# One planner task for both products' chunks of an out tile while attention runs, and two pacing constants of weight narrowing lowered

## The chip, the cores and the metric

The kernel runs on one core of one Trainium2 chip, with float32 inputs and outputs. The metric is the device time of one execution in microseconds; the median of three runs of the kernel before is 704.17 us (703.85 to 704.71).

## What is computed

Three parts follow one another, the output of each being the input of the next. Cut to what matters:

```python
scores = where(causal, -1e9, scale * q @ k.T + minimum(bias, 0))    # 2 x 8 heads, 576 tokens, 64 wide
attn = softmax(scores) @ v                                          # -> x, 1152 tokens x 512
for e in range(4):                                                  # first layer
    h = maximum(x @ w1[e], 0)                                       # 512 -> 1024
    y += p[:, e:e+1] * (h @ w2[e])                                  # 1024 -> 512
g = y @ w_gate                                                      # second layer, 512 -> 1536
out = (g * sigmoid(g) * (y @ w_val)) @ w_out
```

## The kernel before, in words

Large products run on TensorE in a reduced float32 format. To keep float32's precision, each operand is split into a high part and a low part, and a product is three matmuls: high by high, high by low, low by high. `xh` and `xl` are the parts of attention's output, `wah` and `wal` those of an inward weight, `woh` and `wol` of an outward weight, `hh` and `hl` of hidden values. A split is a cast to the high part (lines 326 and 330) and a subtraction for the low part (line 339).

The layers are cut into stages. A stage is one unit of 256 hidden columns for a range of tokens: first the inward products, whose results become hidden values, then `outof` (lines 1170 to 1211), which makes an out tile for every 128 tokens. An out tile sums two chunks of 128 hidden columns (NF = 2), three matmuls each (lines 1184 to 1186), and is then added to `acc_a` or `acc_b` (line 1282 on VectorE, line 1278 on ScalarE for the first).

Inward products have two forms. While attention runs, stages are direct (`into`, lines 1022 to 1024): 256 tokens (EARLY) until the first part of attention is there, 512 (HALF) later. A direct stage of 512 tokens has 24 matmuls of 512 columns. Afterwards a stage is a scheme of seven half-size products (lines 1123 to 1125; the sums of the parts on VectorE are lines 1142 and 1163); for 512 tokens that is 42 matmuls of 256 columns. It needs sums of token halves of x (line 1062, tiles `te` and `tt`), which are formed during and right after attention.

Attention, a pair of heads at a time: scores (lines 534 to 549, of which 546 and 549 use 64 rows of the array), bias and row extremes on VectorE (line 568), exponentials on ScalarE (line 577), reciprocals (line 584), normalization on ScalarE (line 334) or GpSimd (line 336) into `ns`, transposes on TensorE (line 628), and the products with the values (line 687).

Second-layer weights are narrowed to a form that is cheap to split: 36 halves, each loaded (line 776), passed through two operations on ScalarE (lines 784, 791) and three on VectorE (lines 788, 794, 797), and stored to memory (line 801).

The order of all of it is set when the program is built. Every piece of work is a task with a cost, its needs and a rank (`Plan.step`), and the planner always takes the task that can start first, then the one of lower rank; the order in which it takes tasks is each engine's instruction order. Work for the planner comes from `jobs` and `stages` (lines 1438 to 1513). `feed` asks for the next stage while fewer than six tasks of TensorE's dense work are open, so the size of a task says how much work is open. `jobs` yields direct stages as long as attention isn't done ("h" not in `late`) and records them in `part`; then it sets the pace of narrowing, and `stages` takes halves by it:

```python
late["pace"] = 2 * n1 - len(part) + sum(t1 < HALF for t1 in part) - CALM - REST
...
if "h" in late:
    passed += 1
    while late["made_n"] * late["pace"] < (passed - CALM) * 36:
        ...
        x[0].make(x[1])
        late["made_n"] += 1
```

Here n1 is 16, the number of first-layer units, and `passed` counts stages after attention. In the kernel before, `part` has five stages (three of 256 tokens, two of 512), so the pace is 32 - 5 + 3 - 5 - 5 = 20.

Of the kernel before, what the change touches and what calls it, by code (L numbers as in the profile page):

```python
# [18 lines left out]
P = 128  # L19
# [4 lines left out]
PIECES = 2  # L24
# [27 lines left out]
TADD = "vp"  # L52
THIGH = "av"
TLOW = "vp"
REST = 5
CALM = 5
LEAD = 6.0
ISSUE = 0.45
DMA_KB = 0.0033
# [53 lines left out]
def pe(c):  # L113
    return max(c / 2400 + 0.015, 0.109)
# [49 lines left out]
class Plan:  # L164
# [8 lines left out]
    def add(self, eng, cost, run=None, deps=(), take=(), give=(), rank=0.0, port="p", mode="r"):  # L173
        t = Task(eng, cost, run, [d for d in deps if d is not None], take, give, rank, port, mode)
        if not t.missing:
            self.ready.append(t)
        return t
# [102 lines left out]
def attention_moe_swiglu(ctx, tc, q_early, q_late, k, v, s, dp, w1, w2, wg, wv, wo, out):  # L280
# [4 lines left out]
    NT, _, DM = out.shape  # L285
# [6 lines left out]
    NF = FU // P  # L292
# [20 lines left out]
    late = {}  # L313
# [4 lines left out]
    def ring(name, n=2):  # L318
        return rings.setdefault(name, Ring(n))
# [606 lines left out]
    def bank(tag):  # L926

        have = [(psw, {"h": 2, "o": 1}[tag])]
        if "ps" in late:
            have.append((late["ps"], {"h": 3, "o": 2}[tag]))  # L930
        order = [p for i in range(4) for p, n in have if i < n]
        p = order[turns[tag] % len(order)]
        turns[tag] += 1
        return p.tile([P, BANK], F32, name=tag, tag=tag, bufs=dict((id(a), n) for a, n in have)[id(p)])
# [55 lines left out]
    def dense_pe(cost, run, deps, **kw):  # L990
        count["rank"] += 1
        t = add("pe", cost, run, list(deps) + [last_pe["t"]], rank=count["rank"], **kw)
        last_pe["t"] = t
        t.dense = True
        open_pe.append(t)
        return t
# [173 lines left out]
    def order(st):  # L1170

        return [t for t in ORDER if st.t0 <= t * P < st.t1]
# [3 lines left out]
    def outof(w, st, t, evac, split=False):  # L1176
        box = {}
        ts = slice(t * P - st.t0, t * P - st.t0 + P)

        def three(f, y, check=False):  # L1180
            op = box["p"][:, y]
            wh, wl = w.ops
            hh, hl = st.hid
            nc.tensor.matmul(op, hh[:, f, ts], wh[:, f, y], start=f == 0, stop=False, skip_group_check=check)  # L1184
            nc.tensor.matmul(op, hh[:, f, ts], wl[:, f, y], start=False, stop=False, skip_group_check=check)  # L1185
            nc.tensor.matmul(op, hl[:, f, ts], wh[:, f, y], start=False, stop=f == NF - 1, skip_group_check=check)  # L1186

        def item(f):
            def run():
                if f == 0:  # L1190
                    box["p"] = bank("o")
                three(f, slice(0, DM), split)

            def make(last):
                deps = w.done[:-(-(f + 1) * PIECES // NF)] + [x for (ff, c0, n), x in st.lows.items() if ff <= f and c0 < (t + 1) * P and c0 + n > t * P]
                give = []
                if f == NF - 1 and t == order(st)[-1]:
                    give = [(st.first, st.ring)] + ([(w.first, w.parts_ring)] if last else [])
                if f == NF - 1 and split:
                    for y in sides:  # L1200
                        evac(dense_pe(3 * pe(DM // 2), lambda y=y: three(f, y, True), deps), box["t"], lambda: box["p"], y)
                    return
                x = dense_pe(3 * pe(DM), run, deps, take=[] if f else [ring("o")], give=give)
                if f == 0:
                    box["t"] = x
                    x.note = lambda: setattr(plan, "filler", None)
                if f == NF - 1:
                    evac(x, box["t"], lambda: box["p"])
                return x
            return make  # L1210
        return [item(f) for f in range(NF)]

    left = {t: n1 for t in range(NT)}
    fresh = set(range(NT))
# [52 lines left out]
    def moe1_out(w, st, e):  # L1267
        items = []

        for t in order(st):  # L1270
            def evac(x, taker, bank_, t=t):
                new = t in fresh
                fresh.discard(t)

                def run(on="v"):
                    sc = pr[:, t, e:e + 1]
                    if on == "a":
                        nc.scalar.mul(acc(t), bank_(), sc)
                    elif new:
                        nc.vector.tensor_scalar(acc(t), bank_(), sc, None, op0=ALU.mult)  # L1280
                    else:
                        nc.vector.scalar_tensor_tensor(acc(t), bank_(), sc, acc(t), op0=ALU.mult, op1=ALU.add)  # L1282

                a = add(choices("av", "bank", DM) if new else "dve", None if new else 0.74, run,
                        [x, last_acc.get(t), late["gates"]], give=[(taker, ring("o"))], rank=prompt())
                last_acc[t] = a
                left[t] -= 1
                if left[t] == 0:
                    turn_x(t, a)
            items += outof(w, st, t, evac)  # L1290
        return items
# [129 lines left out]
    def moe2_out(w, st, first, last):  # L1421
        items = []
        for t in order(st):
            split = last and st.t0 > 0 and t == order(st)[-1]

            def evac(x, taker, bank_, y=slice(0, DM), t=t, split=split):
                def run(on="v"):
                    if first:
                        move(on, acc(t), bank_())
                    else:  # L1430
                        nc.vector.tensor_tensor(acc(t)[:, y], bank_()[:, y], acc(t)[:, y], op=ALU.add)
                deps = [x, last_acc.get(t)] + (turning[st.t0]["turned"] if first else [])
                c = y.stop - y.start
                a = add(choices("av", "bank", c) if first else "dve", None if first else dve(c), run, deps,
                        give=[] if split else [(taker, ring("o"))], rank=prompt())
                last_acc[t] = a
                if last:
                    add("dma", (0.48, 0.00143 * c), lambda: nc.sync.dma_start(out[t, :, y], acc(t)[:, y]), [a], rank=0)
            items += outof(w, st, t, evac, split)
        return items  # L1440

    def jobs():
# [15 lines left out]
        late["last"] = w_in[-1]  # L1458
        late["pace"] = 2 * n1 - len(part) + sum(t1 < HALF for t1 in part) - CALM - REST
        for i in range(i, n1):  # L1460
# [10 lines left out]
    def stages():  # L1471
# [3 lines left out]
        for i, t0, t1, lastone in jobs():  # L1475
# [12 lines left out]
# [3 lines that stand above are left out]
                    x = next(halves_n, None)  # L1491
# [145 lines left out]
```

## Time and profile before

| what | us |
|---|---|
| median of three runs | 704.17 |
| profiled execution | 702.54 |
| span of that execution | 700.7 |
| TensorE (PE) busy | 690.0 |
| weight loads of TensorE (PEld) busy | 600.8 |
| VectorE (DVE) busy | 539.8 |
| GpSimd (POOL) busy | 463.4 |
| ScalarE (ACT) busy | 356.2 |

The span runs from the first to the last instruction of the profiled execution; 1.84 us of its time lie around it. TensorE's matmuls are pipelined and their ends are modelled, so its busy time is an upper estimate, and the distances between starts tell more. The DMA engines moved 78.45 MB and were busy for between none and eight tenths of a slice. Attention lasts to about 124 us, the first layer to about 495 us, and the second layer takes the rest.

### The profile page before, as it was taken

To read this page: it belongs to the slowest core of one execution; us is meant where nothing else is said; L and a number is where in the kernel's file an instruction comes from. 1 tells how busy PE (TensorE), PEld (TensorE's weight loads), DVE (VectorE), ACT (ScalarE), POOL (GpSimd) and SP (SyncE) were. 2 spreads that over 40 slices of the span, in tenths; PEclk is the share of its full clock that TensorE was granted. 3 is DMA by queue.
4 is the path that set the end of the run, shared out by engine and by line. 5 is a ranking of instruction groups with operands and counts; after the bars stand their busy time and mean duration, and the time that the engine had idled before them with its cause. 6 is when DMAs were issued, how large, how long until landed. Compare 5 with 4: busy or idle time off the path is not lost.

```text
span 700.7 us, 11844 instructions
## 1 busy us (share of the span) xinstructions
PE 690.0 (98%) x4240; PEld 600.8 (86%) x4240; DVE 539.8 (77%) x1080; ACT 356.2 (51%) x751; POOL 463.4 (66%) x456
## 2 busy tenths in 40 slices
PE   8999999999999999999999999999999999999997
PEld 6766667788898989898989889988989999999996
DVE  7876756761678898999899998786876777787665
ACT  7888766233454555555646655455555333323110
POOL 3888726673465867577658677699998848484211
PEclk9999999999999999999999999999999999999999
DMA  6785541211144336534545465312022111000003
GB/s 201 256 286 207 156 150 34 64 62 68 47 150 151 123 119 196 174 112 162 185 132 173 177 195 166 102 38 88 1 75 77 61 31 61 32 31 1 1 1 135
DMA packets 30187, 78.45 MB, mean 112 GB/s; under 512 B 3488, under 2 KB 8096, under 8 KB 30128
## 3 DMA queue, kind: packets, MB, share of 16 engines
q1 hardware_dynamic: 29984, 77.56, 33.8%
q8 instruction: 33, 0.54, 0.3%
q14 instruction: 26, 0.21, 0.1%
q10 hardware_dynamic: 144, 0.13, 0.1%
HBM read 65.85 MB, written 11.83 MB: 111 GB/s over the span
## 4 chain that ended last, share of the span: by engine, by line
PE 89%; ACT 4%; DVE 4%; DMA 2%; issue 1%; SPq 0%; DVEq 0%; ACTq 0%
PE o L1184 13%; PE o L1185 12%; PE o L1186 12%; PE h L1123 12%; PE h L1124 12%; PE h L1125 12%; PE po L687 3%; PE tp L628 2%; PE h L1022 2%; PE h L1024 2%; PE h L1023 2%; ACT ns L577 2%; PE sp L546 2%; DVE tt L1062 1%; PE sp L534 1%; DMA d<-rows 1%
## 5 line engine op out<-in xcount | busy, mean ns | idle before, releaser
L1142 DVE TENSOR_TENSOR cc<-cc,h 128x320 f32<-128x320 f32 (+1 forms) x282 | 126.4, 454 | 51.5 <-PE h L1125 43.4
L1184 PE MATMUL o<-woh,hh 128*128 128x512 f32 x397 | 157.4, 396 | 0.4 <-DVE acc_a L1282 0.3
L1186 PE MATMUL o<-woh,hl 128*128 128x512 f32 x397 | 155.0, 390 | 1.1 <-DVE hl L339 1.1
L1185 PE MATMUL o<-wol,hh 128*128 128x512 f32 x397 | 155.8, 392 | 0.0
L339 POOL TENSOR_TENSOR wal<-raw,wah 128x512 fp32r<-128x512 f32 (+1 forms) x58 | 72.7, 1263 | 34.4 <-ACT wah L326 33.0
L1123 PE MATMUL h<-xh,wsh 128*128 128x320 f32 (+1 forms) x312 | 92.8, 297 | 0.1
L1125 PE MATMUL h<-xh,wsl 128*128 128x320 f32 (+1 forms) x312 | 92.4, 296 | 0.0
L1124 PE MATMUL h<-xl,wsh 128*128 128x320 f32 (+1 forms) x312 | 92.4, 296 | 0.0
L1186 PEld LDWEIGHTS o<-woh,hl 128*128 128x128 f32 x397 | 74.6, 188 | 17.9 <-DVE hl L339 1.5
L339 POOL TENSOR_TENSOR hl<-cc,hh 128x512 fp32r<-128x512 f32 (+1 forms) x29 | 43.5, 1499 | 70.2 <-ACT hh L1254 70.1
L1184 PEld LDWEIGHTS o<-woh,hh 128*128 128x128 f32 x397 | 74.6, 188 | 13.2 <-DVE acc_b L1282 0.8
L339 POOL TENSOR_TENSOR wol<-raw,woh 128x512 fp32r<-128x512 f32 x54 | 77.0, 1441 | 11.8 <-ACT woh L326 10.9
L1185 PEld LDWEIGHTS o<-wol,hh 128*128 128x128 f32 x397 | 74.6, 188 | 10.6
L1251 ACT ACTIVATE cc<-cc 128x640 f32<-128x640 f32 (+1 forms) x46 | 32.2, 699 | 87.9 <-DVE cc L1142 87.9
L1123 PE MATMUL h<-xh,wah 128*128 128x320 f32 (+1 forms) x234 | 69.5, 297 | 0.9 <-DVE cc L1142 0.9
L1124 PE MATMUL h<-xl,wah 128*128 128x320 f32 (+1 forms) x234 | 69.2, 296 | 0.0
L1125 PE MATMUL h<-xh,wal 128*128 128x320 f32 (+1 forms) x234 | 69.2, 296 | 0.0
L339 POOL TENSOR_TENSOR wsl<-sf,wsh 128x512 fp32r<-128x512 f32 x44 | 64.2, 1478 | 2.2 <-ACT wsh L326 2.2
L1282 DVE SCALAR_TENSOR_TENSOR acc_b<-o,pr,acc_b 128x512 f32<-128x512 f32 x75 | 55.5, 744 | 7.0 <-PE o L1186 7.0
L1123 PEld LDWEIGHTS h<-xh,wsh 128*128 128x128 f32 x312 | 58.8, 188 | 1.9 <-ACT cc L326 0.3
L1124 PEld LDWEIGHTS h<-xl,wsh 128*128 128x128 f32 x312 | 58.6, 188 | 1.4
L1125 PEld LDWEIGHTS h<-xh,wsl 128*128 128x128 f32 x312 | 58.6, 188 | 0.0
(156 smaller groups left out, 1631.9 us busy)
## 6 DMA issues: line engine op xcount, KB each, us to landing
raw<-in_w SPq DMA_DIRECT2D x42, 512.0 KB, 5.0
n<-hl SPq DMA_DIRECT2D x36, 256.0 KB, 2.3
raw<-n SPq DMA_DIRECT2D x18, 512.0 KB, 3.3
hh<-in_wg SPq DMA_DIRECT2D x12, 512.0 KB, 4.2
hh<-in_wv SPq DMA_DIRECT2D x12, 512.0 KB, 3.9
hh<-in_wo SPq DMA_DIRECT2D x12, 512.0 KB, 3.8
dql<-rows SPq DMA_DIRECT2D x8, 512.0 KB, 4.0
vr<-in_v SPq DMA_DIRECT2D x4, 640.0 KB, 4.5
```

The costliest lines, as they stand in the source:

```text
L339: {"v": nc.vector, "p": nc.gpsimd}[e].tensor_tensor(to, x, f32(y), op=ALU.subtract)
L546: nc.tensor.matmul(sp[j][:, at:at + w], Q[half[j], x], K[half[j], :w], start=True, stop=False)
L687: nc.tensor.matmul(po[half[j], lo - a:e - a], raw[self.pi // 2]["v"][:kn, c, two + j * D:two + j * D + D], self.spot(self.p[j], c, lo, e, ...
L1123: nc.tensor.matmul(hp, wh, h, start=c == 0, stop=False)
L1124: nc.tensor.matmul(hp, wh, l, start=False, stop=False)
L1125: nc.tensor.matmul(hp, wl, h, start=False, stop=c == 1)
L1142: nc.vector.tensor_tensor(part(k), part(x), banks[i], op=ALU.add)
L1184: nc.tensor.matmul(op, hh[:, f, ts], wh[:, f, y], start=f == 0, stop=False, skip_group_check=check)
L1185: nc.tensor.matmul(op, hh[:, f, ts], wl[:, f, y], start=False, stop=False, skip_group_check=check)
L1186: nc.tensor.matmul(op, hl[:, f, ts], wh[:, f, y], start=False, stop=f == NF - 1, skip_group_check=check)
L1251: nc.scalar.activation(src()[:, o], src()[:, o], AF.Relu)
L1282: nc.vector.scalar_tensor_tensor(acc(t), bank_(), sc, acc(t), op0=ALU.mult, op1=ALU.add)
```

## The change

Two constants are lowered, and `outof` puts both chunks of an out tile, six matmuls, into one task of the planner while attention runs; after attention there is a task for each chunk as before.

```diff
--- before.py
+++ after.py
@@ -52,8 +52,8 @@
 TADD = "vp"
 THIGH = "av"
 TLOW = "vp"
-REST = 5
-CALM = 5
+REST = 4
+CALM = 3
 LEAD = 6.0
 ISSUE = 0.45
 DMA_KB = 0.0033
@@ -1185,30 +1185,32 @@
             nc.tensor.matmul(op, hh[:, f, ts], wl[:, f, y], start=False, stop=False, skip_group_check=check)
             nc.tensor.matmul(op, hl[:, f, ts], wh[:, f, y], start=False, stop=f == NF - 1, skip_group_check=check)
 
-        def item(f):
+        def item(f, e):
             def run():
                 if f == 0:
                     box["p"] = bank("o")
-                three(f, slice(0, DM), split)
+                for x in range(f, e):
+                    three(x, slice(0, DM), split)
 
             def make(last):
-                deps = w.done[:-(-(f + 1) * PIECES // NF)] + [x for (ff, c0, n), x in st.lows.items() if ff <= f and c0 < (t + 1) * P and c0 + n > t * P]
+                deps = w.done[:-(-e * PIECES // NF)] + [x for (ff, c0, n), x in st.lows.items() if ff < e and c0 < (t + 1) * P and c0 + n > t * P]
                 give = []
-                if f == NF - 1 and t == order(st)[-1]:
+                if e == NF and t == order(st)[-1]:
                     give = [(st.first, st.ring)] + ([(w.first, w.parts_ring)] if last else [])
-                if f == NF - 1 and split:
+                if e == NF and split:
                     for y in sides:
                         evac(dense_pe(3 * pe(DM // 2), lambda y=y: three(f, y, True), deps), box["t"], lambda: box["p"], y)
                     return
-                x = dense_pe(3 * pe(DM), run, deps, take=[] if f else [ring("o")], give=give)
+                x = dense_pe(3 * (e - f) * pe(DM), run, deps, take=[] if f else [ring("o")], give=give)
                 if f == 0:
                     box["t"] = x
                     x.note = lambda: setattr(plan, "filler", None)
-                if f == NF - 1:
+                if e == NF:
                     evac(x, box["t"], lambda: box["p"])
                 return x
             return make
-        return [item(f) for f in range(NF)]
+        step = 1 if "h" in late else NF
+        return [item(f, f + step) for f in range(0, NF, step)]
 
     left = {t: n1 for t in range(NT)}
     fresh = set(range(NT))
```

With the order that results, `part` has six stages (three of 256 tokens, three of 512), and the pace is 32 - 6 + 3 - 3 - 4 = 22. From line 1213 on, line numbers are higher by two (1282 is 1284, 1235 is 1237, 1278 is 1280).

The first place is TensorE's, in attention between two groups of scores; `sp` are scores, `po` the products with the values, `tp` transposes, `o` an out tile. The piece is of the difference between the two orders:

```order
 L1185 MATMUL o<-wol,hh 128x512
 L1186 MATMUL o<-woh,hl 128x512
+L1184 MATMUL o<-woh,hh 128x512
+L1185 MATMUL o<-wol,hh 128x512
+L1186 MATMUL o<-woh,hl 128x512
+L687 MATMUL po<-p,vr 64x320 x6
+L687 MATMUL po<-p,vr 64x192 x2
+L687 MATMUL po<-p,vr 64x64 x2
 L546 MATMUL sp<-k_108,ql 128x512 x2
 L549 MATMUL sp<-tri,idr 128x128 x2
 L549 MATMUL sp<-tri,idr 128x64 x2
```

The second chunk of the tile follows the first at once, and the products with the values, which came after the next scores, come ahead of them.

The second place is ScalarE's, at the cast of a sum of token parts (`xh` from `te`) in attention; `st` with a number is a head pair's row statistics. Before:

```order
L334 ACTIVATE ns<-ns,st_119 128x512
L1278 ACTIVATE acc_a<-o,pr 128x512
L577 ACTIVATE ns,st_120<-ns,st_120 128x576
L326 CAST xh_126<-te 128x256
L334 ACTIVATE ns<-ns,st_120 128x576
L577 ACTIVATE ns,st_121<-ns,st_121 128x384 x2
```

and now:

```order
L577 ACTIVATE ns,st_119<-ns,st_119 128x512 x2
L1280 ACTIVATE acc_a<-o,pr 128x512
L326 CAST xh_126<-te 128x256
L334 ACTIVATE ns<-ns,st_119 128x512 x2
L577 ACTIVATE ns,st_120<-ns,st_120 128x576
```

The cast stood ahead of the normalization (line 334) of a group of 576 columns; now it stands ahead of both normalizations of a group of two blocks of 512.

The third place is VectorE's, at the end of attention; line 1235 (1237 now) evacuates hidden values of a direct stage, lines 788, 794 and 797 narrow. Before:

```order
L1235 SCALAR_TENSOR_TENSOR hl<-h,hh 128x512 x2
L1235 SCALAR_TENSOR_TENSOR hl<-h,hh 128x320 x3
L1282 SCALAR_TENSOR_TENSOR acc_a<-o,pr,acc_a 128x512 x2
L1235 SCALAR_TENSOR_TENSOR hl<-h,hh 128x320
L1282 SCALAR_TENSOR_TENSOR acc_a<-o,pr,acc_a 128x512 x2
L1142 TENSOR_TENSOR cc<-cc,h 128x256 x5
L1163 TENSOR_TENSOR cc<-cc,h 128x256
L1282 SCALAR_TENSOR_TENSOR acc_b<-o,pr,acc_b 128x512 x2
L788 TENSOR_SCALAR hl<-hl 128x512 x2
L1282 SCALAR_TENSOR_TENSOR acc_b<-o,pr,acc_b 128x512
L794 ISA hl<-hl 128x1024
```

and now:

```order
L1284 SCALAR_TENSOR_TENSOR acc_a<-o,pr,acc_a 128x512 x2
L1237 SCALAR_TENSOR_TENSOR hl<-h,hh 128x512
L788 TENSOR_SCALAR hl<-hl 128x512 x2
L794 ISA hl<-hl 128x1024
L1237 SCALAR_TENSOR_TENSOR hl<-h,hh 128x512
L797 SCALAR_TENSOR_TENSOR hl<-hh,hl 128x512
L794 ISA hl<-hl 128x1024
L797 SCALAR_TENSOR_TENSOR hl<-hh,hl 128x512
L1237 SCALAR_TENSOR_TENSOR hl<-h,hh 128x320 x3
```

Narrowing came after the last direct stage, among the sums of the first stage of seven products; its first two halves now stand among the evacuations of direct stages.

## Rows read from the trace of the kernel before

**Rows 1.** The page, its parts 1 and 2: busy time, and the granted clock by slices.

```profile
span 700.7 us, 11844 instructions
PE 690.0 (98%) x4240; PEld 600.8 (86%) x4240; DVE 539.8 (77%) x1080; ACT 356.2 (51%) x751; POOL 463.4 (66%) x456
...
PEclk9999999999999999999999999999999999999999
```

**Rows 2.** The page, part 4: the chain that ended last, by engine.

```profile
PE 89%; ACT 4%; DVE 4%; DMA 2%; issue 1%; SPq 0%; DVEq 0%; ACTq 0%
```

**Rows 3.** PE's timeline (start, length, instruction) in a direct stage; a group of weight loads.

```profile
117.21 0.40 PE L1022 MATMUL h<-xh,wah 128*128 128x512 f32 x1
...
120.01 0.49 PE L628 MATMUL tp<-ident,ns 128*128 128x128 f32 x3
...
L1022 PEld LDWEIGHTS h<-xh,wah 128*128 128x128 f32 x112 | 21.1, 188 | 1.6
```

**Rows 4.** PE's timeline in a stage of seven products of 256 columns.

```profile
491.40 0.28 PE L1123 MATMUL h<-xh,hh 128*128 128x256 f32 x1
...
493.50 0.37 PE L1123 MATMUL h<-xh,wsh 128*128 128x256 f32 x1
```

**Rows 5.** PE's waits from 44 to 125 and from 480 to 540 (total, times, longest).

```profile
PE tp L628 <- ACT ns L334: 1.1, 2, 0.7
...
PE h L1123 <- DVE cc L1142: 1.4, 3, 0.5
```

**Rows 6.** Timelines of DVE and PE after the end of attention.

```profile
134.92 2.40 DVE L1062 TENSOR_TENSOR tt<-tt,xh 128x320 f32<-128x320 f32 x2
...
140.94 0.39 PE L1186 MATMUL o<-woh,hl 128*128 128x512 f32 x1
141.65 0.50 PE L1184 MATMUL o<-woh,hh 128*128 128x512 f32 x1 [0.33 <-DVE acc_a L1282]
```

**Rows 7.** Timelines of DVE and PE from 411 to 418, then groups over the span (mean ns).

```profile
412.11 1.70 DVE L794 CUSTOM_DVE_ANT_0 hl<-hl 128x1024 uint16<-128x1024 uint16 x1
...
415.45 1.90 DVE L339 TENSOR_TENSOR hl<-cc,hh 128x640 fp32r<-128x640 f32 x1
...
417.41 0.50 PE L1186 MATMUL o<-woh,hl 128*128 128x512 f32 x1 [1.08 <-DVE hl L339]
...
L797 DVE SCALAR_TENSOR_TENSOR hl<-hh,hl 128x512 int32<-128x512 int32 x36 | 38.4, 1066 | 0.0
L794 DVE CUSTOM_DVE_ANT_0 hl<-hl 128x1024 uint16<-128x1024 uint16 x36 | 34.4, 954 | 0.7
...
L339 DVE TENSOR_TENSOR hl<-cc,hh 128x640 fp32r<-128x640 f32 (+1 forms) x17 | 18.5, 1089 | 0.6 <-ACT hh L1254 0.4
```

**Rows 8.** Groups of GpSimd's work on weights over the span.

```profile
L339 POOL TENSOR_TENSOR wol<-raw,woh 128x512 fp32r<-128x512 f32 x54 | 77.0, 1441 | 11.8 <-ACT woh L326 10.9
...
L330 POOL TENSOR_SCALAR woh<-raw 128x512 fp32r<-128x512 f32 x12 | 7.7, 645 | 5.5 <-PE o L1186 5.5
```

**Rows 9.** Windows: stretch, length, then busy us (count) of PE, PEld, DVE, ACT, POOL; clock.

```profile
44.00:120.00 76.00, 74.89 (x501) 51.10 (x500) 49.38 (x173) 58.19 (x142) 49.35 (x65) 1.00 0.48 155
120.00:140.00 20.00, 20.00 (x99) 15.44 (x98) 13.96 (x18) 5.88 (x14) 14.08 (x15) 1.00 0.21 58
...
350.00:400.00 50.00, 50.00 (x291) 44.60 (x291) 47.00 (x76) 29.06 (x51) 33.65 (x27) 1.00 0.51 168
```

**Rows 10.** PE's timeline in attention, around out tiles.

```profile
44.77 0.40 PE L1186 MATMUL o<-woh,hl 128*128 128x512 f32 x1
45.09 1.13 PE L546 MATMUL sp<-k,ql 64*128 64x512 f32 x4
...
54.99 0.66 PE L628 MATMUL tp<-ident,ns 128*128 128x128 f32 x4 [0.72 <-ACT ns L334]
```

**Rows 11.** ACT's timeline at the wait of the last row above.

```profile
53.85 0.41 ACT L326 CAST xh<-te 128x256 fp32r<-128x256 f32 x1 [1.06 <-POOL te L1062]
```

## The prediction, on record before the change was run

> **What bounds the kernel now.** I read the page first, then TensorE's waits, then its timeline at the places where it waits, and last the engines that it waits for. The page gives TensorE 690.0 of 700.7 us, and the granted clock is in the top tenth in all forty slices [rows 1]. The chain of waits that ended last lies 89% on PE [rows 2]. The modelled busy time of matmuls proves little, so look at their starts: twelve products of 512 columns start from 117.21 to 120.01, which is 2.80 / 12 = 0.2333 us each, with no gap [rows 3], and eighteen of 256 columns from 491.40 to 493.50, 2.10 / 18 = 0.1167 us each [rows 4]. So a column costs the same in either form, and from about 44 us on time goes only into columns, plus a handful of waits. Those after that point are two on ScalarE's normalized scores, 1.1 together, one of 0.33 on an accumulator at 141.65, one of 1.08 at 417.41 and three on VectorE's sums, 1.4 together [rows 5 to 7]. Everything that this change can win lies in those waits and in the drain and refill of TensorE around them, and the waits add up to 3.9 us. A difference under 0.2% (1.4 us: 702.76 to 705.58) can't be told from no change here.
>
> **The change, part by part.** It has three effects on the order.
>
> *One more direct stage.* With both chunks in one task, six open tasks hold more work, so work is made further ahead, and attention ends one stage later in the list: six direct stages, where there were five. The sixth (256 hidden columns, 512 tokens) was a stage of seven half-size products. In the order that is 24 more products of 512 columns in lines 1022 to 1024, 24 x 0.2333 = 5.60 us [rows 3], and 42 fewer of 256 columns in lines 1123 to 1125, 42 x 0.1167 = 4.90 us [rows 4]. All of it is on the engine that sets the end: **+0.70 us**. VectorE loses seven sums with it, which cost nothing either way where TensorE isn't waiting for them. The weights of the sixth stage are now split by GpSimd instead of ScalarE: four pieces, each a high part of 0.645 us and a low part of 1.441 us [rows 8], some 4 x 2.09 = 8.3 us more for GpSimd during attention. That engine is busy for 49.35 of 76.00 us there [rows 9], so the load fits in its idle time of 26.65, and I cost it at nothing; if that cover is gone it shows as the wait of rival B. SyncE issues two weight loads more ahead of a later pair's inputs; the buffers for them come free earlier than those inputs are needed, and I cost this at nothing too.
>
> Here a rule of the Trainium skill speaks otherwise. The weight load of such a product lasts 188 ns of the 233 [rows 3], and the loads fill 86% of the span [rows 1]. The Trainium skill, "Perfetto Trace Analysis", section "Identifying the Most-Contended Engine", calls matmul busy time a bad measure and wants headroom judged by the busy share of weight loads; by it 14% would be open, the extra columns would be taken up, and the sum would lack the 0.70. The trace doesn't agree: the products start every 0.2333 us although their loads are shorter [rows 3].
>
> *Bundles of six.* Out tiles stand between steps of attention as six products instead of three and three. The work is the same. What can differ is (1) the changes between 128-row and 64-row products, and (2) how long TensorE has something to do while the softmax of a group of scores runs. For (1): from 44.77 to 45.09 is 0.32 us, 0.09 more than 0.2333 [rows 10]. The order has 54 such crossings where there were 56: 2 x 0.09, of which I take **-0.1** (bounds -0.2 and 0). For (2): I counted the products that stand between a group's scores and its transposes, each by its start as in [rows 3]. For the groups of 576 columns the order before has 3.18 us at the least, at three of eight places, and only one of these waited: there ScalarE stood 1.06 us at the cast `xh<-te` for GpSimd's sums before it could normalize [rows 11]. The new order has 3.18 at four places, and the largest is 4.57 where it was 4.35; the groups of two blocks of 512 have 4.04 at the least, where one had 3.09. The same cast now stands ahead of both norms of such a group (second piece of order in the change's section). So I cost the waits of attention at **0**, with bounds of -1.1 (both waits of [rows 5] go) and +1.5 (two more like the 0.72 of [rows 10]).
>
> *End of attention and narrowing.* Before, VectorE had a run of sums at 132 to 142 us, two of them 1.20 us each in the row [rows 6], and an out tile's accumulation came late behind them: 0.33 us of wait. In the new order these sums stand singly or in twos between the accumulations. I take **-0.3** there, with bounds of -0.5 (the wait goes with its refill) and +1.0 (the next such evacuation is late by one slow sum).
> Narrowing: CALM and REST make it begin after 4 passed stages instead of 6 and go at 36 / 22 = 1.64 halves a stage, where it was 36 / 20 = 1.80. But attention takes one stage more with it, so in the list of stages it begins one stage sooner and ends at the same place before layer 2. The first halves now come between evacuations of direct stages: 1.07 + 0.95 + 1.07 = 3.1 us of VectorE stand ahead of evacuations that a later out tile reads [rows 7]. Twelve out products (2.80 us) and six inward ones (1.40) cover that, and VectorE is busy there for 13.96 of 20.00 us [rows 9]. I take **0**; uncovered it is +0.8, if each of the three takes 1.7 us as at 412.11 (5.1 less 4.2, rounded down for the part already begun).
> The wait of 1.08 at 417.41 stays: VectorE's order around it (line 794, an accumulation, line 797, then the low part of the hidden values) is the same in the new order, and so is GpSimd's. It comes from length: line 794 takes 1.70 us there against a mean of 0.954, the low part 1.90 against 1.089 [rows 7], both beside GpSimd. I take **0**, bounds -1.2 (the pieces fall apart in time) and +1.2 (a second such place). The three waits of 1.4 at the entry to layer 2 I leave as they are [rows 5]; VectorE and ScalarE do the same things there, with one sum given to GpSimd.
>
> The sum: 0.70 - 0.1 + 0 - 0.3 + 0 + 0 = +0.3 us. The profiled execution took 702.54 (its span 700.7 and 1.84 around it), so the same execution would take 702.84. The median of the runs is 704.17, 1.63 above it; the prediction is for such a median: 704.17 + 0.3, about **704.5**.
>
> **The rivals.**
> *A, faster.* VectorE is the second busiest engine, 47.00 of 50 us at 350 to 400 [rows 9]. Narrowing drawn out by 10% (1.64 for 1.80) loosens its queue there, so that line 794 no longer falls just before the low part at 415. Then that wait goes (-1.2), with the wait at 54.99 (0.72) and the one at 141 (-0.5): 0.70 - 0.1 - 1.2 - 0.72 - 0.5 = -1.8, or **702.4**. For it: one slow pair makes the whole of the 1.08. Against it: the same operations stand in the same order at that place.
> *B, slower.* The queue of ScalarE: seven casts `xh<-te` stand ahead of norms, each waits for sums that GpSimd makes, and GpSimd has 8.3 us more to do in this stretch. If three of them hold the norms as one does now (1.06 of standing, 0.72 of it on TensorE [rows 10, 11]), that is 2 x 0.72 = +1.44, and the gain at 141 does not come if the late groups move into that stretch: 0.70 - 0.1 + 1.44 = +2.0, or **706.2**. It decides from the point where the third sum of a set ends later than the reciprocal of the scores that the norm needs. For it: the cast now holds a norm of two lanes. Against it: most groups have as much cover as before, and GpSimd is idle for a third of the time.
> A rule that would sharpen B is in the Trainium skill, "SBUF — State Buffer", section "Who interferes with whom": a VectorE instruction with two inputs from SBUF and a GpSimd instruction that reads SBUF hold each other up. The rows at 412 to 417 agree with it (1.70 against 0.954) without showing who held whom.
> *C, the change doesn't do what it says.* Begun sooner in number but at nearly the same place, narrowing changes nothing, and the wait at 141 is only moved: 0.70 - 0.1 = +0.6, **704.8**.
> *D, the extra columns are free*, by the rule on weight loads above: -0.1 - 0.3 = -0.4, **703.8**. The starts speak against it [rows 3, 4].
>
> **How the numbers follow.** The forecast has 0.45, A 0.20, B 0.20, C 0.11 and D 0.04. Forecast, C and D lie within 0.2% of no change, but for a little: their bounds of +-1.2 at 415 and -1.1 at the transposes reach past 1.4 now and then. So within 0.2% is 0.60 less 0.03 = 0.57, faster 0.20 + 0.01 = 0.21, slower 0.20 + 0.02 = 0.22. The forecast's own range is 703.3 to 705.5 (704.5 with the bound of -1.2 below and that of +1.0 above). To leave out no more than 2 in 10, the range reaches down to A's 702.4 and up to B's 706.2; half of A and half of B lie outside.
>
> **What the profile of the changed kernel would show.** TensorE's products: 24 more in lines 1022 to 1024, 42 fewer in lines 1123 to 1125, and the same starts, 0.2333 and 0.1167 us. If TensorE's waits on line 334's norms come to about 1.1 after 44 us again, the cover is as I count it; over 2 with the cast of `xh<-te` standing before them is B. No wait on the accumulator at the end of attention shows the term of -0.3 right. A wait on line 339's `hl` of about 1.1, some 415 us from the start, shows that it stayed; its absence is A. What would make all this wrong: a new wait on a buffer or on a load from memory during attention, which no row of the kernel before has.

## The result and the profile after

The changed kernel takes **708.45 us** in the median of seven runs (707.03 to 709.67), the kernel before 704.17 (702.96 to 707.13, seven runs). The ratio is 1.0058 with a 95% interval of 1.0039 to 1.0077: slower by about 4 us, and outside the range that was given. The profiled execution took 709.12.

The page and TensorE's waits, over the whole span (total, times, longest):

```profile
span 707.3 us, 11791 instructions
PE 693.0 (98%) x4222; PEld 600.8 (85%) x4222; DVE 536.4 (76%) x1077; ACT 355.8 (50%) x751; POOL 466.8 (66%) x457
...
PEclk9999999999999999999999999999999999999999
...
PE 80%; DVE 8%; ACT 5%; DMA 4%; issue 2%; POOL 1%; SPq 0%; DVEq 0%; POOLq 0%; ACTq 0%
...
raw<-in_w SPq DMA_DIRECT2D x44, 512.0 KB, 4.4
...
PE tp L628 <- ACT ns L334: 2.1, 5, 0.6
...
PE o L1184 <- DVE acc_b L1284: 1.4, 3, 0.9
PE o L1186 <- DVE hl L339: 1.1, 1, 1.1
PE h L1123 <- DVE cc L1142: 1.0, 2, 0.5
PE o L1184 <- DVE acc_a L1284: 0.9, 2, 0.7
PE sp L534 <- DVE st L568: 0.9, 1, 0.9
PE h L1123 <- ACT cc L326: 0.8, 1, 0.8
```

The clock is as before, but the share of PE in the chain has fallen from 89% to 80% [rows 2], and VectorE, ScalarE and loads have taken it. Three rows of waits are new: on `acc_b`, on `st` in attention and on ScalarE's `cc`. SyncE issues 44 loads of first-layer weights where there were 42. The windows say where the time went (length, busy us of PE, PEld, DVE, ACT, POOL, clock, share and rate of DMA); the first line is the kernel before's, the others are the changed kernel's:

```profile
300.00:350.00 50.00, 50.00 (x300) 45.07 (x299) 45.61 (x75) 28.07 (x50) 33.70 (x27) 1.00 0.46 154
...
140.00:160.00 20.00, 19.29 (x93) 15.99 (x92) 18.08 (x26) 5.85 (x13) 16.80 (x18) 1.00 0.17 54
300.00:350.00 50.00, 47.95 (x278) 42.30 (x278) 41.38 (x67) 23.35 (x42) 32.04 (x25) 1.00 0.44 148
350.00:400.00 50.00, 49.66 (x288) 43.72 (x287) 46.20 (x69) 29.85 (x54) 35.50 (x28) 1.00 0.46 150
```

TensorE lacks 2.05 us at 300 to 350, where it was busy for 50.00 of 50 us in the kernel before, as in the 50 us after it [rows 9]. What happened there is told by four engines, read from the top down (SyncE's queue, ScalarE, VectorE, TensorE):

```profile
328.09 2.37 SPq L825 DMA_DIRECT2D raw<-in_w  x2
330.52 0.42 SPq L776 DMA_DIRECT2D hh<-in_wo  x1
...
337.92 0.66 ACT L784 ACTIVATE hl<-hh 128x512 f32<-128x512 f32 x1 [4.59 <-DMA hh<-in_wo]
...
338.61 0.43 DVE L788 TENSOR_SCALAR hl<-hl 128x512 int32<-128x512 int32 x1 [3.41 <-ACT hl L784]
...
341.12 0.39 PE L1123 MATMUL h<-xh,wsh 128*128 128x256 f32 x1 [0.83 <-ACT cc L326]
```

A half for narrowing is loaded behind two 512 KB loads of weights, and the first operation on it starts 7.4 us after its issue. That operation, on ScalarE, stands at the head of its queue for 4.59 us, with a weight's cast and a sum's copy behind it; VectorE's first operation stands for 3.41 us with accumulations behind it. In attention there is another such place, on VectorE and TensorE:

```profile
51.00 0.72 DVE L499 TENSOR_TENSOR d<-d,tri 128x64 f32<-128x64 f32 x1 [4.07 <-DMA d<-rows]
...
52.78 1.29 PE L534 MATMUL sp<-k,ql 128*128 128x512 f32 x4 [0.88 <-DVE st L568]
```

The sum on a head pair's bias (line 499) waits for its load, and the row extremes of the next group (line 568) wait behind it. In the kernel before, these row extremes were issued ahead of the sum.

### The profile page after: what moved, and what is told of

Read it like the earlier page. It is cut to its first block, busy times and chain, and to the rows that moved or that the text cites. A ratio compares the mean times of both kernels' runs of the same rounds, so it can differ in the third digit from the quotient of the medians.

```text
span 707.3 us, 11791 instructions
## 1 busy us (share of the span) xinstructions
PE 693.0 (98%) x4222; PEld 600.8 (85%) x4222; DVE 536.4 (76%) x1077; ACT 355.8 (50%) x751; POOL 466.8 (66%) x457
## 2 busy tenths in 40 slices
DMA packets 30475, 79.50 MB, mean 112 GB/s; under 512 B 3520, under 2 KB 8128, under 8 KB 30416
## 4 chain that ended last, share of the span: by engine, by line
PE 80%; DVE 8%; ACT 5%; DMA 4%; issue 2%; POOL 1%; SPq 0%; DVEq 0%; POOLq 0%; ACTq 0%
PE h L1123 11%; PE o L1184 11%; PE h L1124 11%; PE h L1125 11%; PE o L1185 11%; PE o L1186 11%; PE po L687 2%; PE tp L628 2%; ACT ns L577 2%; DMA d<-rows 2%; PE h L1022 2%; PE h L1023 2%; PE h L1024 2%; DVE tt L1062 1%; PE sp L546 1%
## 5 line engine op out<-in xcount | busy, mean ns | idle before, releaser
L1142 DVE TENSOR_TENSOR cc<-cc,h 128x320 f32<-128x320 f32 (+1 forms) x276 | 123.9, 454 | 49.5 <-PE h L1125 41.9
L339 POOL TENSOR_TENSOR wal<-raw,wah 128x512 fp32r<-128x512 f32 (+1 forms) x60 | 75.2, 1262 | 40.2 <-ACT wah L326 34.8
L1123 PE MATMUL h<-xh,wsh 128*128 128x320 f32 (+1 forms) x304 | 90.7, 298 | 0.9 <-ACT cc L326 0.8
L1125 PE MATMUL h<-xh,wsl 128*128 128x320 f32 (+1 forms) x304 | 90.2, 297 | 0.0
L1124 PE MATMUL h<-xl,wsh 128*128 128x320 f32 (+1 forms) x304 | 90.2, 297 | 0.0
L339 POOL TENSOR_TENSOR wol<-raw,woh 128x512 fp32r<-128x512 f32 x56 | 80.1, 1446 | 12.1 <-ACT woh L326 11.1
L339 POOL TENSOR_TENSOR hl<-cc,hh 128x512 fp32r<-128x512 f32 (+1 forms) x27 | 40.1, 1486 | 61.7 <-ACT hh L1256 61.6
L1123 PE MATMUL h<-xh,wah 128*128 128x256 f32 (+1 forms) x228 | 67.9, 298 | 0.6 <-DVE cc L1142 0.5
L1124 PE MATMUL h<-xl,wah 128*128 128x256 f32 (+1 forms) x228 | 67.6, 296 | 0.0
L1125 PE MATMUL h<-xh,wal 128*128 128x256 f32 (+1 forms) x228 | 67.6, 296 | 0.0
```

The lines of the kernel that those rows point to most:

```text
L339: {"v": nc.vector, "p": nc.gpsimd}[e].tensor_tensor(to, x, f32(y), op=ALU.subtract)
L1123: nc.tensor.matmul(hp, wh, h, start=c == 0, stop=False)
L1124: nc.tensor.matmul(hp, wh, l, start=False, stop=False)
L1125: nc.tensor.matmul(hp, wl, h, start=False, stop=c == 1)
L1142: nc.vector.tensor_tensor(part(k), part(x), banks[i], op=ALU.add)
```

## The experiments

My first theory was that narrowing's new place makes its loads land late, and that bundles cost one to two microseconds in attention. The rival was that the extra direct stage shifts everything after it, whatever the constants. Each run below was timed against the kernel before on the same chip.

**One part of the change at a time.** `bundle_old_place`:

```diff
-REST = 4
-CALM = 3
+REST = 5
+CALM = 4
```

> The changed kernel with CALM 4 and REST 5: bundles of six and the sixth direct stage stay, narrowing begins after the same stage of the whole list as in the kernel before and goes at the same 36/20. Theory (the narrowing's new place makes its loads land late, and VectorE and ScalarE stand at them at 315 to 390 us): no such waits there, and only the extra columns (+0.7) and attention's waits (+1 to +1.5) stay: 705.5 to 706.5. Rival (the bundles and the sixth stage shift all that follows, whatever the constants): 708 to 709.

708.42 us, ratio 1.0052 (1.0035 to 1.0068): all of the loss without the new place. TensorE's waits between 300 and 372 are gone in its profile, as the theory had it, but others stand in their place (they follow under the spread at the old place). `single_new_place` is the kernel before with CALM 4 and REST 4:

> The kernel before with CALM 4 and REST 4: chunks are single tasks and there are five direct stages, but narrowing has the changed kernel's place in the list and its pace of 36/22. Theory: the waits of 315 to 390 us appear here too, +2.5 to +3.5: 706.7 to 707.7. Rival: no change against the kernel before, 704.2.

703.88 us, ratio 0.9992 (0.9979 to 1.0004): nothing. So my theory fell as an account of the loss: the new place alone costs nothing, and the rival had the right side.

**The sixth stage and the bundles apart.** `single_six_stages` is the kernel before with more open tasks during attention and CALM 4, `bundle_five_stages` the changed kernel whose feeding stops after five stages, with CALM 5 and REST 5:

```diff
-        while sum(t.end is None for t in open_pe) < 6:
+        while sum(t.end is None for t in open_pe) < (6 if "h" in late else 9):
```

> The kernel before (a task for each chunk) with nine open tasks instead of six while attention runs, and CALM 4: attention's products stand as before, but the sixth direct stage is there, narrowing at its old place. Theory (the sixth stage costs its columns and a little at attention's end, the bundles cost the rest): 704.1 + 0.7 + 0.3 = 705.1. Rival (the sixth stage is what costs, its columns and what it shifts later): 707 to 708.5.

```diff
+            late["n"] = len(part) + 1
...
-        while sum(t.end is None for t in open_pe) < 6:
+        while ("h" in late or late.get("n", 0) < 5) and sum(t.end is None for t in open_pe) < 6:
```

> The changed kernel without its sixth direct stage: no new stage is asked for in attention after the fifth, CALM and REST are 5 and 5 as before, bundles of six stay, and every engine's order in attention is the changed kernel's. Theory (bundles cost some 2 to 3 us in attention, at waits on a bias's load and on ScalarE's norms): 706 to 707. Rival (the sixth stage costs all): 704.1.

The two took 705.77 us (ratio 1.0047, 1.0028 to 1.0065; single runs from 704.68 to 710.15) and 703.89 (ratio 1.0002, 0.9994 to 1.0011). The rival was right again: bundles by themselves cost nothing that can be measured, and the sixth stage costs something even without them, 2.1 us by the medians and 3.3 by the ratio. Three of the nine runs, at 708.85 to 710.15, show a mean granted clock of 0.994, and the other six, at 704.68 to 705.97, one of 0.999 or 1.0; the median of the six is 705.35, 1.7 us above the kernel before in the same round. To close the square, `bundle_five_new_place` is the five-stage kernel with CALM 4 and REST 4, the change without its sixth stage:

> Bundles of six, five direct stages, and narrowing at the changed kernel's place and pace (CALM 4, REST 4 with five stages): the whole change without its sixth direct stage. Theory (the sixth stage is what the change loses by): 703.5 to 704.5. Rival (narrowing's new place costs 2 to 3 us once bundles stand before it): 706 to 707.

704.03 us, ratio 0.9998 (0.9986 to 1.0011), as the revised theory had it. Together:

| | five direct stages | six direct stages |
|---|---|---|
| a task for each chunk, old place | 1 (before) | 1.0047 |
| a task for each chunk, new place | 0.9992 | not run |
| bundles, old place | 1.0002 | 1.0052 and 1.0061 |
| bundles, new place | 0.9998 | 1.0058 and 1.0066 (the change) |

Every kernel with six stages is slower, none with five is. The old place holds in stages passed, not at its end: with bundles, the last operation of line 797 falls at 464.91 with six stages and at 441.48 with five. The loss of about 4 us is also not made of the same parts at the two places: TensorE's waits between 300 and 372 stand in neither kernel with six stages at the old place, and in no kernel with five, so they come only with the sixth stage and the new place together.

**The change's bundles with the constants of before.** `bundle_alone` has CALM 5 and REST 5:

> The changed kernel with CALM 5 and REST 5, the constants of the kernel before: bundles alone, which bring the sixth stage with them, so that narrowing begins a stage later. Theory: 706 to 709, as at the other places; rival (the loss belongs to narrowing's earlier begin): 704.1.

714.13 us, ratio 1.0140 (1.0119 to 1.0160), far beyond what either theory had. With a stage fewer after attention and a pace of 19, narrowing ends too late: the last operation of line 797 in the kernel before, in the change and in this run, then this run's waits of TensorE from 470 to 500, and a window there (length, busy us of PE, clock, share and rate of DMA):

```profile
440.70 0.73 DVE L797 SCALAR_TENSOR_TENSOR hl<-hh,hl 128x512 int32<-128x512 int32 x1
...
434.43 0.73 DVE L797 SCALAR_TENSOR_TENSOR hl<-hh,hl 128x512 int32<-128x512 int32 x1
...
480.50 0.68 DVE L797 SCALAR_TENSOR_TENSOR hl<-hh,hl 128x512 int32<-128x512 int32 x1
...
PE h L1125 <- POOL hh L339: 1.8, 2, 1.5
PE o L1312 <- DVE xl L1323: 1.5, 1, 1.5
PE h L1123 <- ACT hh L326: 1.2, 1, 1.2
...
480.00:490.00 10.00, 7.03 (x30) 0.83 0.23 81
```

It finishes 40 us later than before, as the second layer's weights are wanted; TensorE waits at their parts, and in these 10 us the granted clock averages 0.83. So the lowered constants are needed with the sixth stage: they take back some 5.7 of the 10 us that it would cost. An end at 464.91, as above, still left TensorE without waits from 470 to 500. That an end at about 480 is too late was seen once more in a run that was meant for something else, `late_load_planned`:

```diff
-            head = add("act", 0.67, one, [first], rank=rank)
+            head = add("act", 0.67, one, [add(None, 3.0, None, [first])], rank=rank)
```

> The changed kernel with 3.0 us of pretended latency in the planner between a half's load and its first operation on ScalarE, so that the operations are queued later; nothing else is added. Theory (narrowing's operations stand at the head of ScalarE's and VectorE's queues while their load is under way): ScalarE's waits on these loads fall from 26 us between 140 and 480 to a few, and TensorE's waits at 315 to 390 go, -2.5 to -3.5: about 705.5. Rival (VectorE simply has too much to do there): no change, 708.4.

716.47 us, ratio 1.0169 (1.0146 to 1.0192). The waits of 315 to 370 did go, but narrowing's last operation moved to 479.08, and TensorE waited 6.3 us for a part of a second-layer weight. It can't decide on the late loads.

**The two standing places.** `swap_bias_add` and `load_ahead` move one instruction each in the changed kernel's queues and leave all else as it is (the bias sum behind the next two calls of line 568; the two weight loads behind the load of the half). The first:

```diff
-                {"v": nc.vector, "p": nc.gpsimd}[on].tensor_tensor(y, y, f32(tri[:, P:]), op=ALU.add)
+                go = lambda: {"v": nc.vector, "p": nc.gpsimd}[on].tensor_tensor(y, y, f32(tri[:, P:]), op=ALU.add)
+                if pi == 10:
+                    late["hold"] = [2, go]
+                else:
+                    go()
...
+                    if "hold" in late:
+                        late["hold"][0] -= 1
+                        if not late["hold"][0]:
+                            late.pop("hold")[1]()
```

> The changed kernel with one instruction moved on VectorE: the sum of line 499 that waits 4.07 us for the load of a bias (at 51.00 us) is issued behind the next two row extremes of line 568 instead of ahead of them, as it stood in the kernel before. Theory (bundling let it pass ahead, and the scores behind it were late): TensorE's wait of 0.88 at 52.78 goes and those at 55.8 and 58.6 shrink, -1 us: about 707.4. Rival (the exponentials are late for another reason, or a later wait takes the gain): 708.4.

707.19 us, ratio 1.0030 (1.0016 to 1.0045): 1.3 us less than the changed kernel, with an interval below that of the change's second timing (1.0055 to 1.0078, further down), though it overlaps the first (1.0039 to 1.0077). The profile, taken at 705.83, can be laid beside the change's first profile product for product. The change's product at 346.38 follows, then this run's at the two waits of the change:

```profile
346.38 0.50 PE L1184 MATMUL o<-woh,hh 128*128 128x512 f32 x1 [0.85 <-DVE acc_b L1284]
...
51.75 0.59 PE L538 MATMUL sp<-k,ql 128*128 128x512 f32 x1
...
343.38 0.50 PE L1192 MATMUL o<-woh,hh 128*128 128x512 f32 x1
```

The wait of 0.88 is gone, and TensorE is 1.03 us ahead at that place (51.75 for 52.78); 0.7 of it is left after the waits at 55.8 and 58.6, which did not shrink as expected. The other 2 us of the 3.0 at 346 come from the half's load, on which the first operation starts 5.3 us after the issue in this execution and 7.4 in the change's. So by its profile the move is worth 0.7 to 1.0 us. The same move in the five-stage kernel, `bundle_five_swap`:

> As the bundle with five stages, and with line 499's sum issued behind the two row extremes, as in the run that moved it in the changed kernel. Theory: 1.2 us less than without the move, 704.8 to 705.8; were the move worth its gain only beside the sixth stage (the rival), the same as without it.

703.28 us, ratio 0.9991 (0.9982 to 0.9999), is 0.6 us under 703.89, half of what was expected, and the two intervals overlap. For the half's load I first profiled the change again, `changed_again`:

> The changed kernel itself once more, for a second profile. Theory (the waits at 315 to 350 us in its first profile belong to one late load in that execution, since a kernel with the same order there had none): 708.4, and no waits of 1 us at 339.9 and 345.1. Rival (they belong to the order): the same waits at the same places.

708.51 us, ratio 1.0066 (1.0055 to 1.0078). The wait at 339.9 was gone, but the one at 345.1 had stayed (344.07 here), so neither side was quite right. ScalarE's wait for this load in the second profile and in the run with the bias sum moved, whose order here is the same (its lines are numbered higher by eight):

```profile
336.87 0.67 ACT L784 ACTIVATE hl<-hh 128x512 f32<-128x512 f32 x1 [3.59 <-DMA hh<-in_wo]
...
334.89 0.67 ACT L792 ACTIVATE hl<-hh 128x512 f32<-128x512 f32 x1 [2.51 <-DMA hh<-in_wo]
```

Three executions, one order: 4.59, 3.59 and 2.51 us, with TensorE waiting 2.2, 1.8 and at most 0.2 us between 300 and 372. From 300 us to the place of the wait VectorE's durations agree within 0.02 us in all three. How late the load lands behind a megabyte of weights changes from run to run, and this is part of the spread of the changed kernel. So I moved it, `load_ahead`:

```diff
+HOLD = (32, 33)
...
                 nc.sync.dma_start(box["r"], self.w[a].bitcast(I32))
+                for go in late.pop("hold", []):
+                    go()
...
+            late["raws"] = late.get("raws", 0) + 1
+            if late["raws"] in HOLD:
+                late.setdefault("hold", []).append(self.fetch)
...
```

> The changed kernel with one load moved in SyncE's queue: the load of the half at 330.5 us is issued ahead of the two 512 KB weight loads that it stood behind, nothing else differs. Theory (landing behind 1 MB of weights it came 1 to 3 us too late in both profiles, and VectorE and ScalarE stood at it): VectorE's wait at line 788 there goes, TensorE's waits around 340 to 345 go with it, about -2 us: 706.5. Rival (VectorE is late there anyway, or the weights become the late ones): 708.4.

706.93 us, ratio 1.0038 (1.0023 to 1.0054): 1.5 us less, somewhat under the 2 that were expected, just below the interval of the second timing and overlapping that of the first. SyncE's queue and ScalarE there, then TensorE's waits from 300 to 372 in this run and in the change:

```profile
328.26 0.87 SPq L777 DMA_DIRECT2D hh<-in_wo  x1
329.23 1.36 SPq L835 DMA_DIRECT2D raw<-in_w  x2
...
333.35 0.67 ACT L787 ACTIVATE hl<-hh 128x512 f32<-128x512 f32 x1
...
PE o L1194 <- DVE acc_b L1294: 0.5, 1, 0.5
...
PE o L1184 <- DVE acc_b L1284: 1.4, 3, 0.9
PE h L1123 <- ACT cc L326: 0.8, 1, 0.8
```

ScalarE no longer waits for this load, and 1.7 of 2.2 us of TensorE's waits are gone. Product for product TensorE is level with the change's first profile up to 339 us (within 0.2) and 2.4 us ahead from 370 on, all of it at the places of these waits. `both_moves` makes the two moves together:

> The changed kernel with both moves, the sum of line 499 behind two row extremes on VectorE and the load of the half ahead of two weight loads on SyncE. Theory (two separate waits): 1.25 and 1.5 us add up, 705.7; what is left against five stages (704.0) is then 1.7, the sixth stage's 0.7 of columns and about 0.9 of the accumulator's wait at 154. Rival (the two are one delay handed on, or a later wait takes the gain): about 707, as with either.

705.26 us, ratio 1.0024 (1.0014 to 1.0035), an interval below both of the change's. Within the noise the two add up: 3.2 us less by the medians, where the single moves give 2.8; 2.4 less by the ratios, where they give 3.4. What is left, 1.7 us by the ratio and 2.2 by the medians, fits the sixth stage's 0.7 of columns and one wait that I didn't move, the accumulator's at the end of attention (VectorE, then TensorE, in the changed kernel):

```profile
152.97 0.98 DVE L339 TENSOR_TENSOR xl<-tt,xh 128x320 fp32r<-128x320 f32 x1
153.88 0.48 DVE L1062 TENSOR_TENSOR tt<-tt,xl 128x320 f32<-128x320 f32 x1
154.28 1.40 DVE L1284 SCALAR_TENSOR_TENSOR acc_a<-o,pr,acc_a 128x512 f32<-128x512 f32 x2
...
155.07 0.50 PE L1184 MATMUL o<-woh,hh 128*128 128x512 f32 x1 [0.71 <-DVE acc_a L1284]
```

It is 0.71 us where it was 0.33 [rows 6], and in the five-stage bundles it isn't there at all. The accumulation stands behind VectorE's sums of token halves. The one at 153.88 takes 0.48 us; one of the same form at 148.55, while GpSimd works on a weight's low part (148.38 to 149.79), took 1.58. That this wait makes up the rest is argued, not shown.

**The spread at the old place.** `bundle_old_place` had a first profile at 705.82, 2.6 us under its median, so it was profiled again, `bundle_old_place_again`:

> The changed kernel with CALM 4 and REST 5 for a second profile, since its first profiled execution was its fastest (705.82, median 708.42). Theory: a profile at 707 to 709 shows the missing 2 to 3 us at a late load of a half or of weights, with waits of TensorE right behind it that the first profile lacks. Rival: it is spread over the span.

708.84 us, ratio 1.0061 (1.0038 to 1.0084); its span is 707.1, against 704.0 of the first profile. At 198 us it is already 1.4 us behind that profile, after a wait of 0.8 in attention (line 534 on line 568) that the first didn't have. The rest comes just after layer 2 begins. TensorE's timeline and the windows (busy us, clock) of the second profile:

```profile
508.46 0.31 PE L1125 MATMUL h<-xh,hl 128*128 128x320 f32 x1
510.64 0.43 PE L1123 MATMUL h<-xh,hl 128*128 128x320 f32 x1 [1.87 <-ACT cc L326]
...
512.20 0.47 PE L1123 MATMUL h<-xh,hh 128*128 128x320 f32 x1
512.46 0.47 PE L1124 MATMUL h<-xl,hh 128*128 128x320 f32 x1
...
510.00:512.00 2.00, 1.36 (x6) 0.73 0.35 88
512.00:514.00 2.00, 2.00 (x9) 0.50 0.43 174
514.00:516.00 2.00, 2.00 (x14) 0.92 0.00 0
```

The wait of 1.87 us on ScalarE's copy, which stood behind a cast that waited for GpSimd's sums, is in both profiles (1.89 in the first). In the second the granted clock then falls to 0.50, its lower level, and products of 320 columns start every 0.27 us instead of 0.147 for some 3.5 us, which costs about 1.5. In the first it stayed at 1.00. Neither theory nor rival had this: there is no late half in it, and the difference lies in two places. The fall of the clock is common at the old place: of the fifteen runs of the two timings ten, all at 708.08 or more, show a mean granted clock of 0.996 or 0.997, and five, from 705.82 to 707.46, one of 0.999 or 1.0. All thirteen runs of the changed kernel show 0.999 or 1.0. So about 3 of the 4.3 us at the old place come without the clock, and the changed kernel pays its loss wholly without it.

## Why the prediction was wrong

**One more direct stage** is the step that failed: "I cost it at nothing", said of the weights' splits, "I cost this at nothing too", said of their loads, and so 0.70 us for the whole stage. The columns came out as counted (24 more, 42 fewer; 6 products of 512 columns still start in 1.40 us, 151.41 to 152.81). But the stage has other costs. Beside bundles it measured 1.0058 against 0.9998, 4.2 us. I also read the weights wrongly: they aren't split by GpSimd in place of ScalarE; a direct unit's second token range comes much later as a stage of its own, so the unit's weights are loaded and split **a second time** (44 loads for 42, 79.50 MB for 78.45). In the changed kernel GpSimd has 56 low parts and 14 high parts of outward weights where it had 54 and 12 [rows 8], and as many more of inward weights, 8.5 us together; ScalarE's casts of outward weights are 42 in both:

```profile
L339 POOL TENSOR_TENSOR wol<-raw,woh 128x512 fp32r<-128x512 f32 x56 | 80.1, 1446 | 12.1 <-ACT woh L326 11.1
...
L326 ACT CAST woh<-raw 128x512 fp32r<-128x512 f32 x42 | 24.6, 618 | 16.8 <-PE o L1186 16.8
...
L330 POOL TENSOR_SCALAR woh<-raw 128x512 fp32r<-128x512 f32 x14 | 9.1, 650 | 3.4 <-PE o L1186 3.3
```

GpSimd had the idle time for that, as I said; what shifted is where loads and sums fall against each other, with three results:

- *End of attention*: -0.3 was taken, and a wait of 0.71 us was measured where 0.33 had been. The bound of +1.0 held it. In the five-stage bundles the wait did go.
- *Narrowing*: 0 was taken, with +0.8 as the price uncovered. I priced VectorE's busy time, 3.1 us ahead of an evacuation, and not the load that its operations stand at. Measured: 2.2 and 1.8 us of TensorE's waits between 300 and 372; one move of a load took back 1.5 in the median. The pace and the place as such were harmless, as forecast: 0.9992 and 0.9998 with five stages. That narrowing ends at about the same place held too (434.43 and 440.70).
- *Layer 2's entry*: 0 was taken; the rows of 1.4 [rows 5] became 1.0 on `cc`. At the old place it was the dear one (1.87 on ScalarE, and the clock).

These parts make up most of the loss. By the starts of TensorE's products in the first profile, the accumulator's wait costs 0.87 us (153.97 to 155.07 less one product of 0.2333), and the waits at 320, 341, 346 and 370, taken in the same way, cost 2.85 together. With 0.70 of columns and 0.4 given back at layer 2's entry that is 4.0 of the 4.2 us.

**Bundles of six** were right in sum and partly wrong in mechanism. 0 was taken for attention's waits, and the ratio measured with five stages was 1.0002. But TensorE's waits in attention came to 2.2 us in the changed kernel and 2.1 in `bundle_five_stages`, where the profile before had 1.1 [rows 5]: 1.3 on norms, the rest on a bank that row extremes had not freed. Of this 0.33 came back at 141; the rest is not accounted for, and it may not belong to the bundles. In `single_new_place`, which has the kernel before's order in attention, the waits of 44 to 125 were 2.3 us:

```profile
PE tp L628 <- ACT ns L334: 1.8, 2, 1.4
PE tp L628 <- POOL ns L336: 0.5, 1, 0.5
```

So executions of one order differ by as much as was to be explained. The -0.1 for crossings is smaller than any of these runs could show. I had looked at ScalarE's cast as the head of a queue (rival B); the one that came was on VectorE, at a bias's load that was even waited for before (1.41 us, by VectorE's timeline at 49.24), when nothing urgent stood behind it. A new wait in attention that goes back to a load was the prediction's last sign of being wrong, and it showed. B's time of 706.2 was the nearest of the rivals, by another mechanism.

**The wait at 417** stayed, 1.1 us, as forecast; A, which needed it gone, is out. **C** was right that narrowing's place changes little, and wrong that the change then costs 0.6. **D** is out. The Trainium skill, "Perfetto Trace Analysis", section "Identifying the Most-Contended Engine", judges headroom by the busy share of weight loads. They fill 85% of the span now, and the open 15% took up none of the extra columns.

What stays open: which part of the sixth stage's cost is the second loading of its weights and which the shift alone; where the clock fell in three of nine runs of `single_six_stages`, of which there is no profile; and whether the accumulator's wait is the last 1 us after both moves.

## What to carry to other kernels

In a list-scheduled kernel, count what an option makes the planner *ask for*, not only what it reorders: a bigger task moved a stage across a phase boundary, and that stage brought a second load of its weights. Price an operation that is moved by the load it stands at and by what lies ahead of that load in the queue; an operation that waits at the head of an in-order engine costs what stands behind it, however little it does itself. And undo side effects one at a time before judging a change: here the named change was worth nothing that could be measured, and its side effect cost all.

## What was not expected of the hardware

With the same order of the queues there, one 512 KB load issued behind two others took 5.3, 6.4 and 7.4 us from its issue to the first operation on it, and VectorE's wait at line 788 grew with it, 1.34, 2.40 and 3.41 us. And in one of two executions of the same kernel a wait of 1.87 us, seven microseconds after one of 0.73, was followed by a granted clock of 0.50 for some 3.5 us; in the other a wait of 1.89, as long after one of 0.63, left the clock at 1.00.
